# Attention's five key chunks and first 64 queries weighed in one stretch, and one copy of q moved to ScalarE

## The chip, the cores and the metric

The program runs on one core of a Trainium2 chip. The metric is the device time of one execution in microseconds (us), as a median over runs. TensorE (PE) multiplies, VectorE (DVE), ScalarE (ACT) and GpSimd (POOL) do the element work, and SyncE (SP) issues most of the DMAs. Each engine works off its own queue in the order in which the program was written, and waits for the others through semaphores.

## The reference

Three layers follow each other. The change lies in the first one alone.

```python
scores = (1.0 / np.sqrt(D)) * np.matmul(q, k.transpose(0, 1, 3, 2))   # B, H, S, D = 4, 8, 576, 64
mask = (pos[:, None] // 64) >= (pos[None, :] // 64)                   # causal by blocks of 64
scores = np.where(mask, scores, -1e9)
scores = scores - np.max(scores, axis=-1, keepdims=True)
attn = np.exp(scores)
attn = attn / (np.sum(attn, axis=-1, keepdims=True) + 1e-09)
x = np.matmul(attn, v)                     # then laid out as [B*S, H*D] = [2304, 512]
...                                        # mixture of 8 experts: each token goes to its argmax expert
...                                        # last layer: x @ w_in, a piecewise activation, @ w_out
```

## The kernel before, in words

Attention works on 16 pairs of heads, pair n = 0 to 15 (batch n // 4, two heads at a time, one head per half of the 128 partitions). Each pair goes through seven steps z = 0 to 6. Step z of pair n computes the scores of one piece of queries (`scores`), reduces their maximum on DVE and takes the exponential on ACT (`soft`, lines 344, 339 and 348 for the maximum, 350 for the exponential into `pall`). Two steps later (`LAG = 2`) `flip` transposes that piece on PE (line 368) into a PSUM tile `pt`, and ACT (line 379) or DVE (line 511) copies it to `pT`. So the last two pieces of a pair are flipped in steps 0 and 1 of the next pair. The piece that is flipped last, in step 1, is copied by ACT.

Work that is not part of this chain is placed by the table `PLAN`: its key (z, at) names the step and the place in it, `act` runs what is listed there.

```python
PLAN = {(1, 0): ["rows", "q"], (2, 0): ["sum"], (2, 2): ["k", (0, 3)], (3, 0): ["rows"],
        (4, 2): [(3, 5)], (5, 0): ["first"], (5, 1): ["store"], (6, 2): ["rows"]}
```

- "q" is `load_q` of the next pair: PE transposes q (`psq`), ACT copies it out scaled (`qT`, line 256) and casts it (`qa`, line 259, two halves); DVE (lines 265, 266) and POOL (lines 263, 260, 267, 268) make the further forms of q. Line 266 is a copy of 64 columns on 64 partitions.
- "k" is `load_k` of the next pair: PE transposes k (`psk`), DVE copies it out (`kT`, line 286) and casts two parts of `kd` (line 297), ACT casts the two others (line 295), POOL subtracts the low part `kl` in two halves (line 298).
- a pair of numbers is `weigh` of the pair before: for these chunks of 128 keys PE multiplies `pT` with v into `px` (line 393), the two heads in the two halves of the 128 output partitions, each matmul as two passes in the trace. Chunk 0 covers 512 queries, the others 448, 320, 192 and 64.
- "first" is `weigh_first` of the pair before: the first 64 queries against chunk 0 (`py`, line 408, in a tile of the two `pt` buffers), then, where the pair before is odd, `row_order`, and a copy on ACT (line 412). `row_order` is small copies of the reciprocal row sums on DVE (line 429, one or two; line 435, two).
- "sum" (DVE lines 417 and 418), "store" (ACT line 398, which empties `px`) and "rows" (PE line 445, DVE lines 451 and 455) finish the rows of the pairs before.

An even pair n is one in which the pair before is odd, so it carries "sum" and `row_order`; that is n = 2, 4, 6, 8, 10, 12 and 14. Where the batch of the pair before is odd (n = 6, 8, 14) line 429 runs twice, else once. Pairs 14 and 15 also carry the routing of the experts on DVE. After attention come the experts and the last layer, which make up the other three quarters of the time.

Of the kernel before, what the change touches and what calls it, by code (L numbers as in the profile page):

```python
# [49 lines left out]


ORDER_FIRST, ORDER_LAST, ORDER = (2, 4, 0, 1, 5, 6, 3), (3, 1, 4, 2, 6, 0, 5), (3, 1, 0, 4, 2, 6, 5)
PLAN = {(1, 0): ["rows", "q"], (2, 0): ["sum"], (2, 2): ["k", (0, 3)], (3, 0): ["rows"],
        (4, 2): [(3, 5)], (5, 0): ["first"], (5, 1): ["store"], (6, 2): ["rows"]}
FROM = 0, 128, 256, 320, 448
LAG = 2
COPY = 4
# [65 lines left out]
def attention(late, weights, tc, q, k, v, ids, w_gate, mbias, x_dram, dram, ident, tabs):  # L123
# [3 lines left out]
    nc = tc.nc  # L127
# [54 lines left out]
    def turned(dst, x):  # L182
        if x.dtype == F32R:
            nc.tensor.transpose(dst.bitcast(F32R), x, identr)
        else:
            nc.tensor.transpose(dst, x, ident)
# [58 lines left out]
    def eng(n, x):  # L245
        return nc.gpsimd if SMALL[n > 0][x] == 2 else nc.vector

    def load_q(n):
        psq = ps2.tile([P, 1024], F32, tag="big", name=f"psq{n}")
        psq = psq[:, 64:64 + S]  # L250
        for t, x in enumerate(FROM):
            turned(psq[:, x:x + P], io_t[n, "q"][:, t, :])
        qa, qb, qf = qas[n % 2], qbs[n % 2], qfs[n % 2]

        qT = wk.tile([P, 9, 64], F32, tag="qT", name=f"qT{n}", bufs=1)
        nc.scalar.activation(qT, psq.rearrange("p (i t) -> p i t", t=64), AF.Copy, scale=D ** -0.5)
        for h in range(2):
            hs, oh = slice(h * 64, h * 64 + 64), slice(64 - h * 64, 128 - h * 64)
            nc.scalar.copy(qa[hs, h, :7], qT[hs, 2:])
            eng(n, h).tensor_tensor(qa[oh, h, :7], qT[hs, 2:], qa[hs, h, :7].bitcast(F32), op=ALU.subtract)  # L260
        for h in range(2):
            hs = slice(h * 64, h * 64 + 64)
            (nc.gpsimd.tensor_copy if n else nc.scalar.copy)(
                qf[hs, h].rearrange("p (i t) -> p i t", t=64), qT[hs, :2])
        eng(n, 4).tensor_copy(qb[:64, :7], qa[:64, 0, :7])
        eng(n, 5).tensor_copy(qb[64:, 7], qa[64:, 1, 6])
        eng(n, 6).tensor_copy(qb[64:, 8:], qa[64:, 1, :6])
        eng(n, 7).tensor_copy(qzs[n % 2][:, 64:], qa[:, 1, 6])

# [199 lines left out]
    def act(n, z, at):  # L469

        if n >= B * NP:
            return
        for what in PLAN.get((z, at), ()):
            if what == "q" and n + 1 < B * NP:
                load_q(n + 1)
            elif what == "k" and n + 1 < B * NP:
                load_k(n + 1)
            elif what == "rows" and todo:
                done.add(todo[0])
                rows(*todo.pop(0))  # L480
            elif n == 0:
                continue
            elif isinstance(what, tuple):
                weigh(n - 1, *what)
            elif what == "sum" and (n - 1) % 2:
                row_sums((n - 1) // NP, (n - 1) % NP // 2)
            elif what == "first":
                weigh_first(n - 1)
            elif what == "store":
                store_xT(n - 1)  # L490
                if (n - 1) % 2:
                    todo.extend((j, (n - 1) % NP // 2) for j in rows_of[(n - 1) // NP])

    warm(WARM[0])
    load_k(0)
    load_q(0)
    warm(WARM[1])
    for g in range(len(steps) + LAG):
        n, z = divmod(g, NK)
# [1081 lines left out]
```

## Time and profile before

| what | value |
|---|---|
| median of 3 runs | 840.74 us (840.67 to 841.1) |
| the profiled execution | 839.69 us |
| its span, first to last instruction | 837.8 us |
| granted TensorE clock, mean | 0.992 |
| PE, PEld, DVE, ACT, POOL busy | 98%, 85%, 73%, 59%, 25% |
| chain that ended last | PE in 46% of the span, DVE, issue and DVE's sequencer 0% |

The times of runs are device times; the rows of the trace count from the first instruction of the profiled execution. PEld is the weight load of TensorE, which overlaps its matmuls. A matmul's end is modelled, so the distance between the starts of two matmuls tells more than their durations. Where a row says x5, five instructions of the same kind were merged, and the second number is the time from the first start to the last end.

### The profile page before, as it was taken

To read this page: it belongs to the slowest core of one execution; us is meant where nothing else is said; L and a number is where in the kernel's file an instruction comes from. 1 tells how busy PE (TensorE), PEld (TensorE's weight loads), DVE (VectorE), ACT (ScalarE), POOL (GpSimd) and SP (SyncE) were. 2 spreads that over 40 slices of the span, in tenths; PEclk is the share of its full clock that TensorE was granted. 3 is DMA by queue.
4 is the path that set the end of the run, shared out by engine and by line. 5 is a ranking of instruction groups with operands and counts; after the bars stand their busy time and mean duration, and the time that the engine had idled before them with its cause. 6 is when DMAs were issued, how large, how long until landed. Compare 5 with 4: busy or idle time off the path is not lost. (4 is left out here: it accounts for less than half of the span.)

```text
span 837.8 us, 13997 instructions
## 1 busy us (share of the span) xinstructions
PE 817.9 (98%) x4936; PEld 709.3 (85%) x4936; DVE 608.3 (73%) x1115; ACT 495.6 (59%) x994; POOL 205.4 (25%) x249
## 2 busy tenths in 40 slices
PE   6999999998899999999999999999999999999998
PEld 5777777775788888888888999999999988888887
DVE  6788888789666656797873766766636877777774
ACT  5898888896533334464544666766657644444442
POOL 8546556546301212120202000110000011112120
PEclk6999999999999999999999999999999999999999
DMA  6445655630744447765625453453644633333301
GB/s 155 119 125 144 172 145 134 171 95 20 247 131 150 153 125 234 240 204 163 203 84 162 142 176 121 170 175 134 218 120 160 239 143 128 125 126 126 132 32 38
DMA packets 138058, 123.17 MB, mean 147 GB/s; under 512 B 70183, under 2 KB 122423, under 8 KB 135296
## 3 DMA queue, kind: packets, MB, share of 16 engines
q1 hardware_dynamic: 132256, 107.98, 41.9%
q0 software_dynamic: 4384, 13.92, 4.7%
q8 instruction: 40, 0.66, 0.3%
q10 hardware_dynamic: 1344, 0.33, 0.2%
q14 instruction: 34, 0.28, 0.1%
HBM read 89.17 MB, written 40.37 MB: 155 GB/s over the span
## 5 line engine op out<-in xcount | busy, mean ns | idle before, releaser
L1019 PE MATMUL h<-yhi,wi 128*128 128x384 f32 x768 | 200.4, 338 | 1.1 <-ACTq L1253 1.1
L1019 PEld LDWEIGHTS h<-yhi,wi 128*128 128x128 f32 x768 | 139.5, 188 | 1.5 <-ACTq L1253 1.5
L1019 PE MATMUL h<-ylo,wi 128*128 128x384 f32 x384 | 129.2, 337 | 0.0
L1293 ACT ACTIVATE cl<-h,half 128x384 f32<-128x384 f32 x96 | 55.9, 582 | 69.4 <-PE h L1019 69.1
L350 ACT ACTIVATE pall<-s,nmax 128x384 f32<-128x384 f32 (+2 forms) x144 | 79.5, 558 | 28.1 <-DVE nmax L344 17.0
L1297 DVE SCALAR_TENSOR_TENSOR gg<-cl,h 128x384 f32<-128x384 f32 x96 | 52.3, 552 | 51.8 <-ACT cl L1294 49.7
L1423 PE MATMUL p<-wo,s 128*128 128x256 f32 (+1 forms) x432 | 87.8, 338 | 0.0
L1423 PEld LDWEIGHTS p<-wo,s 128*128 128x128 f32 x432 | 68.5, 188 | 9.2
L1478 POOL DMA_INDIRECT out_dram<-rest,tab x16 | 27.3, 1707 | 190.9 <-DVE rest L1445 185.4
L1019 PEld LDWEIGHTS h<-ylo,wi 128*128 128x128 f32 x384 | 72.1, 188 | 0.0
L368 PE MATMUL pt<-ident,pall 128*128 128x128 f32 x400 | 65.7, 282 | 5.5 <-DVE pT L511 3.5
L1423 PE MATMUL p<-wo,a 128*128 128x256 f32 (+1 forms) x330 | 66.0, 335 | 0.0
L1019 PE MATMUL h<-xhi,wh 128*128 128x512 f32 (+2 forms) x164 | 63.1, 385 | 0.0
L1019 PE MATMUL h<-xhi,wl 128*128 128x512 f32 (+2 forms) x164 | 61.7, 376 | 0.5 <-DVE wl L1103 0.5
L1019 PE MATMUL h<-xlo,wh 128*128 128x512 f32 (+2 forms) x164 | 61.6, 376 | 0.0
L1128 PE MATMUL acc<-wh,hl 128*128 128x512 f32 x152 | 59.6, 392 | 0.1
L1423 PEld LDWEIGHTS p<-wo,a 128*128 128x128 f32 x330 | 52.8, 188 | 7.9
L1128 PE MATMUL acc<-wl,hh 128*128 128x512 f32 x152 | 59.3, 390 | 0.0
L1128 PE MATMUL acc<-wh,hh 128*128 128x512 f32 x152 | 59.1, 389 | 0.0
L393 PE MATMUL px<-pT,v 128*64 128x448 f32 (+4 forms) x320 | 54.5, 432 | 0.0
L1294 ACT ACTIVATE cl<-cl 128x384 f32<-128x384 f32 x96 | 50.5, 526 | 3.0
L368 PEld LDWEIGHTS pt<-ident,pall 128*128 128x128 f32 x400 | 43.9, 143 | 7.0 <-issue 3.1
(316 smaller groups left out, 1807.8 us busy)
## 6 DMA issues: line engine op xcount, KB each, us to landing
raw<-in_moe_w_dram SPq DMA_DIRECT2D x80, 256.0 KB
g_dram<-gg SPq DMA_DIRECT2D x48, 384.0 KB
g<-g_dram SPq DMA_DIRECT2D x18, 1024.0 KB
wi_raw<-in_moe_w_in_dram SPq DMA_DIRECT2D x16, 512.0 KB
wo_raw<-in_moe_w_out_dram SPq DMA_DIRECT2D x16, 512.0 KB
yr<-y_dram SPq DMA_DIRECT2D x18, 256.0 KB
x_dram<-xrow SPq DMA_DIRECT2D x33, 128.0 KB
v<-in_v_dram SPq DMA_DIRECT2D x32, 128.0 KB
```

What stands on the lines that cost most here:

```text
L350: nc.scalar.activation(pall[n % 2][:, o:o + w], pss[:, u:u + w], AF.Exp, bias=nm[:, x:x + 1], scale=1.0, accum_out=ssum[:, b, c, x:x + 1])
L368: nc.tensor.transpose(pt[:, kk, :], pa[:, o + kk * P:o + (kk + 1) * P], ident)
L393: nc.tensor.matmul(pxs[n][h * 64:(h + 1) * 64, s0 - 64:], io_t[n, "v"][:, kk, h * D:(h + 1) * D], pTs[n][:, kk, h, s0:], start=(kk == 0), ...
L1019: nc.tensor.matmul(ps, a[za], b[zb], start=(i == 0), stop=(i == n - 1))
L1128: nc.tensor.matmul(accs[s][u], a[:, us], b[:, 1, :], start=(f == 0 and i == 0), stop=(f == NF - 1 and i == 2))
L1293: nc.scalar.activation(cl, ph, AF.Relu, bias=half, scale=0.5)
L1294: nc.scalar.activation(cl, cl, AF.Square)
L1297: nc.vector.scalar_tensor_tensor(gg[:, :, f % 2, :], cl.rearrange(t3, t=P), 1.0, ph.rearrange(t3, t=P), op0=ALU.min, op1=ALU.max)
L1423: nc.tensor.matmul(o, a, b, start=(x == 0 and i in FRESH), stop=(x == len(terms) - 1), skip_group_check=True)
L1478: outs.append(nc.gpsimd.indirect_dma_start(out=out[:, :], out_offset=bass.IndirectOffsetOnAxis(ap=tabs.tab[:, j, 0:1].bitcast(U32), axis=0 ...
```

## The change

`PLAN` moves three things: chunks 3 and 4 of `weigh` go from step 4 to step 2, behind chunks 0 to 2; `weigh_first` goes from the start of step 5 to step 2, ahead of `weigh`, and takes `row_order` with it; `store` goes from step 5 to step 3. In `load_q` of all pairs but the first, line 266 goes from DVE to ACT.

```diff
-PLAN = {(1, 0): ["rows", "q"], (2, 0): ["sum"], (2, 2): ["k", (0, 3)], (3, 0): ["rows"],
-        (4, 2): [(3, 5)], (5, 0): ["first"], (5, 1): ["store"], (6, 2): ["rows"]}
+PLAN = {(1, 0): ["rows", "q"], (2, 0): ["sum"], (2, 2): ["k", "first", (0, 5)], (3, 0): ["rows"],
+        (3, 1): ["store"], (6, 2): ["rows"]}
...
         eng(n, 4).tensor_copy(qb[:64, :7], qa[:64, 0, :7])
-        eng(n, 5).tensor_copy(qb[64:, 7], qa[64:, 1, 6])
+        (nc.scalar.copy if n else nc.vector.tensor_copy)(qb[64:, 7], qa[64:, 1, 6])
         eng(n, 6).tensor_copy(qb[64:, 8:], qa[64:, 1, :6])
```

On PE, step 2 of pair 5 to the scores of step 3 (the names carry buffer numbers: psk and px as above, xr the "rows", s_4 the scores of step 3). Before:

```order
L184 MATMUL psk_1149<-identr,k_892 128x128 x5
L393 MATMUL px_1165<-pT_962,v_563 64x512 x2
L393 MATMUL px_1165<-pT_962,v_563 64x448 x2
L393 MATMUL px_1165<-pT_962,v_563 64x320 x2
L445 MATMUL xr_1_1176<-rh,xT 128x144 x2
```

And now:

```order
L184 MATMUL psk_1149<-identr,k_892 128x128 x5
L408 MATMUL py_1165<-pT_962,v_563 64x64 x2
L393 MATMUL px_1169<-pT_962,v_563 64x512 x2
L393 MATMUL px_1169<-pT_962,v_563 64x448 x2
L393 MATMUL px_1169<-pT_962,v_563 64x320 x2
L393 MATMUL px_1169<-pT_962,v_563 64x192 x2
L393 MATMUL px_1169<-pT_962,v_563 64x64 x2
L445 MATMUL xr_1_1184<-rh,xT 128x144 x2
```

All matmuls with 64 output columns of weights stand together now, py ahead; the later stretch of them in step 4 and 5 is gone.

On DVE, the even pair 6 from k's copy to the maximum of its last piece (rt is what `row_order` writes):

```order
 L286 COPY kT_1389<-psk_1383 128x576
 L297 CAST kd_1391<-kT_1389 64x576 x2
-L348 TENSOR_REDUCE nmax_1257<-s_4_1410 128x1
-L511 COPY pT_1374<-pt_1_0_1414 128x2x2x128
-L348 TENSOR_REDUCE nmax_1257<-s_2_1422 128x1
 L429 COPY rt<-rinv 64x4x4 x2
 L435 COPY rt<-rinv 64x2 x2
-L339 TENSOR_REDUCE nmax_1257<-s_6_1444 128x1
+L348 TENSOR_REDUCE nmax_1257<-s_4_1422 128x1
+L511 COPY pT_1374<-pt_1_0_1427 128x2x2x128
+L348 TENSOR_REDUCE nmax_1257<-s_2_1435 128x1
+L339 TENSOR_REDUCE nmax_1257<-s_6_1445 128x1
```

The copies of `row_order` now follow the casts of kd directly, and the maxima of three pieces and a copy of pT stand behind them.

On ACT, two places of step 1 to step 4, pair 6 (pT_1140 is copied in the flip of step 1, which `weigh` waits for). Line 266 now stands between the casts of qa and that copy:

```order
 L256 ACTIVATE qT_1341<-psq_1335 128x576
 L259 CAST qa_137<-qT_1341 64x448 x2
+L266 COPY qb_139<-qa_137 64x64
 L379 COPY pT_1140<-pt_5_0_1359 128x4x128
 L350 ACTIVATE pall_157,ssum<-s_1_1353,nmax_1257 128x256 x2
```

And the two copies into xT (lines 412 and 398) now precede the exponential of step 3 instead of following that of step 4. POOL's queue is unchanged; on SP only buffer numbers differ.

## Rows read from the trace of the kernel before

**Rows 1.** Busy time in stretches: length, PE, PEld, DVE, ACT, POOL, clock, DMA share, GB/s.
```profile
26.00:187.00 161.00, 159.86 (x1231) 121.46 (x1230) 131.69 (x282) 140.50 (x389) 90.63 (x108) 1.00 0.53 136
187.00:222.00 35.00, 28.47 (x237) 21.08 (x238) 28.92 (x92) 21.28 (x58) 19.90 (x28) 1.00 0.38 120
```

**Rows 2.** Timeline of PE in the odd pair 7: start, length, what.
```profile
101.78 2.76 PE L393 MATMUL px<-pT,v 128*64 128x512 f32 x12
...
106.44 0.41 PE L368 MATMUL pt<-ident,pall 128*128 128x128 f32 x2
106.78 0.66 PE L393 MATMUL px<-pT,v 128*64 128x192 f32 x8
...
107.49 0.40 PE L316 MATMUL s<-kd,qa 128*128 128x288 f32 x1
107.73 0.29 PE L316 MATMUL s<-kd,qz 128*128 128x288 f32 x1
107.86 0.29 PE L316 MATMUL s<-kl,qb 128*128 128x288 f32 x1
```

**Rows 3.** Timeline of TensorE's weight loads there; in brackets the idle time before.
```profile
102.17 0.22 PEld L393 LDWEIGHTS px<-pT,v 128*64 128x64 f32 x3 [0.21 <-ACT pT L379]
```

**Rows 4.** Timeline of PE in pair 15.
```profile
205.67 2.37 PE L393 MATMUL px<-pT,v 128*64 128x512 f32 x12
```

**Rows 5.** Timeline of ACT in pair 7.
```profile
108.13 0.20 ACT L412 COPY xT<-py 128x64 f32<-128x64 f32 x1
108.23 0.60 ACT L398 COPY xT<-px 128x512 f32<-128x512 f32 x1
```

**Rows 6.** Timeline of DVE in the even pair 8.
```profile
113.56 0.39 DVE L265 CAST qb<-qa 64x448 fp32r<-64x448 f32 x1 [0.96 <-ACT qa L259]
114.15 0.85 DVE L266 CAST qb<-qa 64x64 fp32r<-64x64 f32 x1 [0.20 <-ACT qa L259]
...
115.75 0.43 DVE L417 TENSOR_SCALAR rinv<-ssum 128x18 f32<-128x18 f32 x1
...
117.45 0.94 DVE L297 CAST kd<-kT 64x576 fp32r<-64x576 f32 x2
118.31 0.68 DVE L348 TENSOR_REDUCE nmax<-s 128x1 f32<-128x512 f32 x1
...
120.09 1.32 DVE L429 COPY rt<-rinv 64x16 f32<-64x16 f32 x2
```

**Rows 7.** Timeline of POOL in pair 8.
```profile
113.71 2.44 POOL L260 TENSOR_TENSOR qa<-qT,qa 64x448 fp32r<-64x448 f32 x2
116.21 0.50 POOL L267 CAST qb<-qa 64x384 fp32r<-64x384 f32 x1
...
118.05 3.10 POOL L298 TENSOR_TENSOR kl<-kT,kd 64x576 fp32r<-64x576 f32 x2 [1.04 <-DVE kd L297]
```

**Rows 8.** Timeline of PE in pair 8: the first 64 queries, the flip of step 5.
```profile
119.64 0.34 PE L408 MATMUL py<-pT,v 128*64 128x64 f32 x4
...
120.81 0.60 PE L368 MATMUL pt<-ident,pall 128*128 128x128 f32 x4
```

**Rows 9.** The copies of lines 429 and 435: ns min/median/max, first and last start.
```profile
L429 DVE COPY rt<-rinv x12: 175/643/1116, 45.0 to 219.2; 64x16 f32<-64x16 f32 x8, 128x16 f32<-128x16 f32 x4
L435 DVE COPY rt<-rinv x16: 151/164/168, 46.0 to 219.6; 64x2 f32<-64x2 f32 x16
```

**Rows 10.** Timeline of PE in pair 0 and in step 0 of pair 7.
```profile
17.93 0.58 PE L326 MATMUL s<-kd,qa 128*128 128x256 f32 x1 [0.72 <-ACT pall L350]
...
97.94 0.33 PE L368 MATMUL pt<-ident,pall 128*128 128x128 f32 x1 [0.33 <-ACT pall L350]
```

**Rows 11.** Timeline of DVE in pair 14, and POOL's kl there.
```profile
194.95 0.94 DVE L297 CAST kd<-kT 64x576 fp32r<-64x576 f32 x2
...
197.84 0.93 DVE L690 TENSOR_TENSOR rk<-rk,oh 128x104 f32<-128x104 f32 x1
...
195.56 3.08 POOL L298 TENSOR_TENSOR kl<-kT,kd 64x576 fp32r<-64x576 f32 x2 [3.51 <-DVE kd L297]
```

## The prediction, before the changed kernel was run

> **What bounds the kernel now.** I read the busy time in stretches first. [...] In the last two pairs (187 to 222 us) PE is busy for 28.5 of 35 us and DVE for 28.9 [rows 1]: there DVE holds PE up.
>
> Next, PE's timeline in an odd pair. The starts show that "busy" hides losses. The two heads of px run side by side in the two halves of the array. In pair 7 the first head's first matmul starts at 101.78 [rows 2], but the second head's weights load only at 102.17, after ACT's copy of pT [rows 3]. The second head ends 0.39 us late and the next work waits for it. So the start of the stretch already hangs on ACT's chain from psq through qT and qa to that copy. The second thing to see is what a stretch of px costs at its edges. Two transposes start at 106.44; by their length, 0.41 for two of 0.27, their spacing is 0.14, and a third would start by 106.69. Instead px, py and the edges last until 107.49, and the first matmul after takes 0.24 to the next, where the one after takes 0.13 [rows 2]: 0.80 + 0.11 = 0.91 us.
>
> Last, DVE, POOL and PE in an even pair. On DVE, the copy of line 266 takes 0.85 us and ends at 115.00, just behind POOL's first subtract (half of 2.44 from 113.71, so 114.93); line 417 ends at 116.18, behind the second (116.15). Line 429 starts at 120.09 and its two copies take 1.32 us, though one alone takes 0.18: POOL's kl runs from 118.05 to 121.15, and the first copy ends only then [rows 6, 7, 9]. So a DVE copy from SBUF to SBUF waits for the POOL instruction that is running, until it ends. Maxima, which read PSUM, do not: that of 118.31 runs its 0.68 us beside kl [rows 6].
>
> **The change, part by part.** The sum is made against the profiled execution (839.69 us), which is 1.05 us below the median of 840.74.
>
> *One stretch instead of two.* The later stretch of 0.91 us goes; its 320 columns per head (192 + 64 of px, 64 of py) now run inside the first. A stretch in which neither head waits takes 2.37 us for 512 + 448 + 320 = 1280 columns with its edges [rows 4], 1.85 ns a column, so they cost at most 0.59. Gain 0.3 us a pair, for pairs 1 to 15.
>
> *py ahead of px.* py takes the `pt` buffer that ACT's copy in step 1 empties, so now both heads wait for it, where only the second did. Since the second head set the end, this costs nothing further. *Line 266 on ACT* stands ahead of that copy and delays it. No row shows it on ACT. The nearest is ACT's copy of 64 columns, line 412: 0.20 us long, 0.10 from its start to that of the next [rows 5]. I take 0.10; the bounds are 0 and 0.28 (one full copy and a hand-over). A gain is excluded, as ACT's queue ahead of it is unchanged.
> Odd pairs 1 to 13: 7 x (-0.3 + 0.1) = **-1.4**. Pair 15 has no later q: **-0.3**.
>
> *The copy off DVE.* In the odd pairs the maxima come up to 0.85 us earlier, and PE waits for none of them. In pair 0 it does: PE idles 0.72 us at 17.93 for an exponential whose maximum stood behind line 266 [rows 10]: **-0.7**.
>
> *The store earlier* empties px sooner; nobody waits for it. Its two copies on ACT, 0.7 us [rows 5], now precede the exponential of step 3, which must wait for later matmuls and a maximum anyway: nothing. DMA issues and POOL's queue do not move.
>
> *row_order in step 2.* This is the dear part. Take pair 8. Without line 266, DVE goes on at 113.95 instead of 115.00, and line 417 waits for POOL's first subtract instead of the second, ending at 114.98 instead of 116.18. What follows moves 1.2 us up to the casts of kd, due at 116.25 instead of 117.45. There POOL runs line 267 (116.21 to 116.71), so the first cast ends near 117.0, the second near 117.5 [rows 6, 7]. kl starts 0.14 after the end of the first cast (118.05 against 117.45 + 0.46), so near 117.15, and its halves of 1.55 us end at 118.7 and 120.25. Line 429 is due at 117.5 and waits for the first half. POOL goes on at once with the second, so the next copy waits for that: 120.3. Two of 0.16 follow: 120.65. Behind them in DVE's queue stands the maximum of step 3, 0.68 us, which now starts at 118.31 [rows 6]; then ACT's exponential, 0.69 by the same number of columns, and hand-overs of 0.1: 122.1. PE's flip of that piece, which started at 120.81 [rows 8], starts 1.3 us later. What PE gains before that point is lost in this wait: the stretch joined, and the 0.3 us by which py ran late in this pair, at 119.64 behind DVE's copy of pT [rows 8]. Pairs 6 and 8 have two copies of line 429: 2 x 1.3. Pairs 2, 4, 10 and 12 have one; the second small copy of line 435 is then the one that meets the second half, and 0.3 us of copies less stands behind it: 4 x 1.0. Sum **+6.6**. What line 429 costs now in step 0 of the next pair, 0.33 us at 97.94 [rows 10] and less in others, goes: **-0.5**.
>
> *Pair 14* has no POOL work beside row_order now, and will have: the casts end at 195.89, kl at 198.64 [rows 11]. With DVE 0.4 earlier the copies end near 198.5, and the next maximum comes 2.7 later than the 195.8 at which it follows the casts now. Given back are 0.7 of copies that stood later and some 0.65 of line 690's 0.93, of which most is the wait for kl [rows 11]: **+1.3**, with bounds of 0 and 2.7.
>
> Sum: -1.4 - 0.3 - 0.7 + 6.6 - 0.5 + 1.3 = **+5.0 us**, so 844.7 by the profiled execution and 845.7 by the median. The chain of pair 8 is worked with no slack at all and a few tenths of it can overlap; I take 0.1 off each of seven pairs: **845.0 us**. After attention PE is the bound up to the end, and what PE loses reaches the end.
>
> [...] The small copies of line 435 never met POOL: all sixteen took 0.15 to 0.17 us [rows 9]. That they wait like line 429 is my reading, by the nearest row: the same operation between the same two tiles. [...] If only what rows show holds, the four pairs with one line 429 fall to the second rival below. [...]
>
> **The rivals.** *First, faster: the copies wait once.* If the rest of the copies slips in between kl's halves, before POOL takes up the second, the maximum of pair 8 starts at 118.7 + 0.04 + 0.5 = 119.25 and the flip at 120.75, even with now; in the four pairs with one line 429 it is 0.2 better than now; pair 14 comes out even. Sum: -1.4 - 0.3 - 0.7 - 0.8 - 0.1 - 0.5 = -3.8, 837 us. For it: a copy that is waiting could bring the next along before POOL goes on. Against: line 417 and line 266, each behind a POOL instruction, show POOL going on at once. It decides by when that maximum starts: PE would reach the flip at about 120.3 (120.81 less 0.3 and 0.3, plus 0.1), and 1.5 us of maximum, exponential and hand-overs lie before it, so from 118.8 on each tenth of delay is a tenth of PE's time.
>
> *Second: only the small copies of line 435 pass.* Then pairs 2, 4, 10 and 12 gain 0.2 instead of losing 1.0: 4.8 less, 840.2 us.
>
> *Third: line 266 on ACT costs 0.28.* The odd pairs lose their gain: 7 x 0.18 = +1.3, 846.3 us.
>
> *Fourth: the loss is taken up later*, in the 35 us where DVE holds PE up [rows 1]: about 841 us. Against: DVE's work of those pairs hangs on the same scores and comes late with them.
>
> **How the numbers follow.** Forecast 0.62, copies wait once 0.16, small copies pass 0.11, ACT dearer 0.05, taken up 0.06. The forecast's own range is 842 to 849: per even pair 0.6 to 1.6 in place of 1.0 to 1.3 (6 x 0.4 either way), pair 14 between 0 and 2.7. The second and fourth rivals lie within 839 to 842; the first, at 837, stays out. So 838.5 to 849.0. A measurement of this kernel can tell about 0.2% from no change, 1.7 us. Faster by more (below 839.1): the first rival and a little of the second, 0.19. Within it (up to 842.4): most of the second and fourth, 0.16. Slower: the forecast and the third, 0.65.
>
> **What would show it.** In the changed profile of pair 8: line 429 merged with a length near 2.5 us or more directly behind the casts of kd, both halves of kl under it; an idle time on PE of 1 to 2 us before a transpose of line 368, put down to ACT's pall, in every even pair; periods of odd pairs 0.2 us shorter; py right behind psk, waiting for ACT's pT. Wrong would be: rt's copies short, or long with no idle PE behind them, or even pairs no longer than now.

## The result, and the profile after

| | before | after |
|---|---|---|
| median | 840.7 us (840.62 to 841.1, 4 runs) | 846.21 us (845.03 to 847.9, 4 runs) |
| profiled execution, its span | 839.69 us, 837.8 us | 847.9 us, 846.1 us |
| granted TensorE clock, mean | 0.992 | 0.988 |
| PE, DVE, ACT, POOL busy | 98%, 73%, 59%, 25% | 96%, 72%, 59%, 24% |

The changed kernel takes 1.0066 times the time of the kernel before (95% interval 1.0049 to 1.0082): slower by 5.5 us. The sum of the prediction was 5.0; its forecast, with 0.7 taken off for overlap, was 845.0 us, 4.3 above the kernel before. The execution whose trace is read below is the longest of the four, 1.7 us above their median.

The busy time in the two stretches of [rows 1], in the changed kernel:

```profile
26.00:187.00 161.00, 144.74 (x1171) 111.72 (x1171) 128.66 (x254) 137.50 (x386) 86.74 (x105) 0.99 0.52 135
187.00:222.00 35.00, 29.98 (x253) 23.53 (x252) 30.91 (x89) 22.64 (x64) 18.68 (x28) 0.90 0.16 49
```

PE, the bound of attention before, now lacks 16.3 of 161 us, and its mean granted clock is no longer 1.00. The two groups of copies of [rows 9] show why (minimum, median, maximum in ns):

```profile
L429 DVE COPY rt<-rinv x12: 176/1292/1307, 40.6 to 226.0; 64x16 f32<-64x16 f32 x8, 128x16 f32<-128x16 f32 x4
L435 DVE COPY rt<-rinv x16: 151/167/1409, 41.8 to 226.4; 64x2 f32<-64x2 f32 x16
```

The median of line 429 doubled, and line 435, never above 0.17 us before, now reaches 1.41. DVE's timeline in pair 8, to be laid beside [rows 6], and POOL's beside [rows 7]:

```profile
114.33 0.39 DVE L265 CAST qb<-qa 64x448 fp32r<-64x448 f32 x1 [0.96 <-ACT qa L259]
114.64 0.68 DVE L344 TENSOR_REDUCE nmax<-s 128x2 f32<-128x512 f32 x1
115.25 0.51 DVE L417 TENSOR_SCALAR rinv<-ssum 128x18 f32<-128x18 f32 x1
...
117.02 1.27 DVE L297 CAST kd<-kT 64x576 fp32r<-64x576 f32 x2
118.30 1.51 DVE L429 COPY rt<-rinv 64x16 f32<-64x16 f32 x2
119.85 1.45 DVE L435 COPY rt<-rinv 64x2 f32<-64x2 f32 x2
121.33 0.69 DVE L348 TENSOR_REDUCE nmax<-s 128x1 f32<-128x512 f32 x1
```

```profile
114.48 2.44 POOL L260 TENSOR_TENSOR qa<-qT,qa 64x448 fp32r<-64x448 f32 x2
...
117.98 3.11 POOL L298 TENSOR_TENSOR kl<-kT,kd 64x576 fp32r<-64x576 f32 x2
```

Four small copies fill 118.30 to 121.30, as long as kl runs on POOL, and the maximum behind them starts only then. PE's timeline of that pair shows who pays, to be laid beside [rows 8]:

```profile
112.32 0.63 PE L184 MATMUL psq<-identr,q 128*128 128x128 f32 x5
...
121.08 0.29 PE L316 MATMUL s<-kl,qb 128*128 128x288 f32 x1
122.88 0.66 PE L368 MATMUL pt<-ident,pall 128*128 128x128 f32 x4 [1.51 <-ACT pall L350]
123.47 0.23 PE L635 MATMUL idp<-ident,idf 18*128 18x18 f32 x1
123.84 0.67 PE L326 MATMUL s<-kd,qa 128*128 128x512 f32 x1
...
128.27 0.63 PE L184 MATMUL psq<-identr,q 128*128 128x128 f32 x5
```

The flip of step 5, at work without a wait before, stands idle for 1.51 us. The same view of line 368 alone, over 26 to 187 us, has six such waits, one in each of the pairs 2, 4, 6, 8, 10 and 12 (before there were two, 0.6 us together, the larger in [rows 10]):

```profile
L368 PE MATMUL pt<-ident,pall x300: 270/273/455, 30.0 to 182.2; 128*128 128x128 f32 x150
its engine sat idle before it (us, times) until:
  ACT pall L350: 7.7, 6
```

In an odd pair the two other parts of the change can be seen, the copy of line 266 on ACT and the joined stretch. ACT's and PE's timelines of pair 7, for [rows 2, 3]:

```profile
100.51 0.65 ACT L256 ACTIVATE qT<-psq 128x576 f32<-128x576 f32 x1 [0.20 <-PE psq L184]
101.19 1.15 ACT L259 CAST qa<-qT 64x448 fp32r<-64x448 f32 x2
102.38 0.24 ACT L266 CAST qb<-qa 64x64 fp32r<-64x64 f32 x1
102.64 0.59 ACT L379 COPY pT<-pt 128x512 f32<-128x512 f32 x1
```

```profile
103.28 0.34 PE L408 MATMUL py<-pT,v 128*64 128x64 f32 x4 [0.61 <-ACT pT L379]
103.45 2.76 PE L393 MATMUL px<-pT,v 128*64 128x512 f32 x20
```

The copy of line 266 takes 0.24 us on ACT and moves the copy of pT by 0.26 (102.38 to 102.64). PE waits for that copy ahead of py, and then runs all five chunks in one piece.

One thing in the profile after was in no step of the prediction. Three stretches of pair 8, with the granted clock in the third column from the right:

```profile
122.00:124.00 2.00, 0.98 (x6) 0.72 (x7) 1.92 (x5) 1.93 (x6) 0.00 (x0) 1.00 0.72 225
124.00:126.00 2.00, 2.00 (x9) 1.48 (x10) 0.69 (x1) 1.26 (x4) 1.51 (x4) 0.50 0.37 148
126.00:128.00 2.00, 2.00 (x13) 1.69 (x12) 1.10 (x4) 0.90 (x3) 0.00 (x0) 0.65 0.00 1
```

Behind the idle 1.51 us the clock is at its lower level, 0.50 of full speed, for 3.41 us from 124.0 on; it is there again from 202.5 (6.83 us) and from 226.4 (3.41 us). From 26 us to the end of attention the kernel before was never at that level (1.00 in both stretches of [rows 1]).

### The profile page after: what moved, and what is told of

Same layout as the page of the kernel before. It is cut to its first block, busy times and chain, and to the rows that moved or that the text cites. A ratio compares the mean times of both kernels' runs of the same rounds, so it can differ in the third digit from the quotient of the medians.

```text
span 846.1 us, 14025 instructions
## 1 busy us (share of the span) xinstructions
PE 810.0 (96%) x4936; PEld 704.0 (83%) x4936; DVE 612.5 (72%) x1100; ACT 499.5 (59%) x1009; POOL 204.8 (24%) x249
## 5 line engine op out<-in xcount | busy, mean ns | idle before, releaser
L1100 ACT CAST wh<-raw 128x1024 fp32r<-128x1024 f32 x40 | 41.9, 1051 | 13.2 <-PE acc L1128 13.1
```

Of the source, the lines that this page charges most:

```text
L1100: nc.scalar.copy(ws[s, f][0], weights.raw[s, f])
```

## The experiments

A pair's period, from the start of the turns of q (line 184) to the next such start, separates the effects better than the total. The table gives it in us for the pairs that alternate. Pairs 6 and 8 stand apart because line 429 has two copies there, pairs 7 and 9 because their periods differ from the other odd ones in the kernel before already. "Idle" is PE's idle time ahead of py and ahead of line 368 between 26 and 187 us; by the kernel's pace 12 to 14 pairs start their stretch in that window. "-" is a value that is left out, as the lower clock falls into it.

| kernel | pairs 3, 5, 11, 13 | 7, 9 | 2, 4, 10, 12 | 6 | 8 | idle py | idle 368 |
|---|---|---|---|---|---|---|---|
| before | 12.12 to 12.13 | 12.61 | 12.47 to 12.64 | 13.11 | 12.94 | 0 | 0.6 |
| after | 12.07 | 12.55 | 13.44 to 13.61 | 13.95 | 15.95 | 8.3 | 7.7 |
| e1 | 12.06 | 12.55 | 12.05 to 12.21 | 12.58 | 12.53 | 8.9 | 0.2 |
| e2 | 11.80 | 12.28 | 14.31 (pair 10) | - | - | 4.3 | 11.2 |
| e3 | 12.39 to 12.41 | 12.89 | 12.39 to 12.56 | 12.55 | 12.76 | 0 | 0 |
| e4 | 12.06 | 12.54 | 12.05 to 12.22 | 12.33 | 12.64 | 8.9 | 0 |
| e5 | 11.78 to 11.81 | 12.28 | 12.48 to 12.63 | 13.10 | 12.95 | 4.6 | 0.9 |
| e6 | 12.34 (13: 12.61) | 12.82 | 13.45 to 13.61 | 13.95 | 14.33 | 12.1 | 6.0 |
| e7 | 11.79 to 11.80 | 12.28 | 11.79 to 11.95 | 12.31 | 12.24 | 5.2 | 0.2 |
| e8 | 12.87 to 12.88 | 12.97 | 13.53 to 13.62 | 14.11 | 14.07 | 0 | 4.0 |
| e9 | 11.68 to 11.69 | 12.15 to 12.16 | 13.30 to 13.34 | 13.81 | 13.76 | 0 | 8.0 |

The kernel before ran beside each group, each group on a chip of its own: 840.48 us for e1 to e4, 837.25 for e5 to e8, 841.08 for e7 once more and e9. Ratios are taken against these. The times expected of e5 to e8 were worked out from runs beside 840.5 to 840.7 us, so there the periods are the better test.

**e1: row_order back at the start of step 5.** Everything else of the change stays.

```diff
-        (3, 1): ["store"], (6, 2): ["rows"]}
+        (3, 1): ["store"], (5, 0): ["order"], (6, 2): ["rows"]}
...
-                weigh_first(n - 1)
+                weigh_first(n - 1, False)
+            elif what == "order":
+                if (n - 1) % 2:
+                    row_order((n - 1) // NP, (n - 1) % NP // 2)
```

> The change with row_order alone put back to the start of step 5. If the even pairs lose their time to row_order's copies behind kl (the theory), their idle time of 1.2 to 1.5 us on PE before the flip of step 5 is gone; even pairs come out some 0.3 us shorter than in the kernel before and odd ones 0.05 shorter, so with the 1 to 1.6 us of pair 0 and 1 some 836 to 838 us. If the loss came from the joined stretch, or from the store and the copy of q on ACT (the rival), nothing changes: 845 to 847 us.

Measured: 833.72 us (832.69 to 834.19), ratio 0.9913 (0.99 to 0.9926). The waits of line 368 are gone but for one, and the copies run at their own length:

```profile
L368 PE MATMUL pt<-ident,pall x325: 270/273/329, 30.0 to 183.9; 128*128 128x128 f32 x163
its engine sat idle before it (us, times) until:
  ACT pall L350: 0.2, 1
```

```profile
L429 DVE COPY rt<-rinv x12: 176/178/183, 43.6 to 212.9; 64x16 f32<-64x16 f32 x8, 128x16 f32<-128x16 f32 x4
L435 DVE COPY rt<-rinv x16: 153/164/167, 43.7 to 213.2; 64x2 f32<-64x2 f32 x16
```

What follows: the copies of row_order, where they stand, are the whole loss and more, and the rest of the change gains. Each even pair is 1.4 us shorter than in the changed kernel (pair 8 by 1.8 against its 14.33 at the full clock in e6), and the mean granted clock of this execution is 1.000 over its 832.0 us. The gain of the rest, 6.8 us, is above the 2.5 to 4.5 that I expected; e3 and e5 split it.

**e2: the new order alone, line 266 back on VectorE.**

```diff
-        (nc.scalar.copy if n else nc.vector.tensor_copy)(qb[64:, 7], qa[64:, 1, 6])
+        eng(n, 5).tensor_copy(qb[64:, 7], qa[64:, 1, 6])
```

> The new table alone, line 266 on DVE as before. By the theory the copy on DVE delays the casts of kd, so kl and row_order's copies come up to 0.9 us later: even pairs lose 1.9 us instead of 1.0, odd pairs gain 0.3; 849 to 852 us. If the copy on ACT is what costs the time (the rival), this is faster than the change: below 845 us.

Measured: 859.75 us (857.62 to 861.43), ratio 1.0225 (1.0207 to 1.0244), worse than the 849 to 852 expected. The waits ahead of the flip of step 5 are longer, 2.10 to 2.45 us, as DVE comes to row_order later. Pair 10, the one even pair from 2 to 12 that ran wholly at the full clock, lost 1.84 us against the kernel before, and 1.9 was expected; what was not expected is the clock. It falls to 0.50 for 3.41 or 6.83 us seven times between 48.0 and 239.1 us (mean of the execution 0.984), five of them in or right behind such a wait. PE's timeline of pair 6, and the stretch behind it:

```profile
103.28 1.11 PE L368 MATMUL pt<-ident,pall 128*128 128x128 f32 x4 [2.45 <-ACT pall L350]
```

```profile
104.00:108.00 4.00, 4.00 (x18) 3.17 (x17) 1.62 (x5) 2.66 (x8) 0.00 (x0) 0.50 0.00 0
```

**e3: line 266 on ScalarE alone, in the old order.**

```diff
-        eng(n, 5).tensor_copy(qb[64:, 7], qa[64:, 1, 6])
+        (nc.scalar.copy if n else nc.vector.tensor_copy)(qb[64:, 7], qa[64:, 1, 6])
```

> The table as before, line 266 on ACT. The copy lies ahead of the copy of pT that the second head waits for: 0.26 us in each odd pair, some 0.1 us gained in each even one where DVE is freed, 0.7 to 1.6 us gained in pair 0 and 1: 840 to 842 us. If the rival holds (the copy is what makes the change slow), 844 to 846 us.

Measured: 839.31 us (837.9 to 841.25), ratio 0.9987 (0.9976 to 0.9997), 0.7 below the theory's window and far from the rival's. Odd pairs are 0.27 us longer, even pairs 0.08 shorter (pair 6 by 0.56, pair 8 by 0.18).

**e4: row_order in step 2 as in the change, but ahead of load_k.**

> The change with row_order still in step 2, but ahead of load_k, so its copies meet POOL's short instructions of q and the casts of kd and kl follow them. By the theory it is kl that they must not stand behind: they wait at most 1 us in all, kd comes about 1 us later, and the maximum of step 3 at most 0.5 us late; 836 to 840 us, no idle time on PE of over 0.6 us before the flip of step 5. If any copies of row_order ahead of that maximum cost the time, wherever they stand (the rival), 845 to 847 us.

The edit puts "order" between the sums and "k" of step 2. Measured: 833.45 us (831.93 to 834.99), ratio 0.9911 (0.9896 to 0.9925), with nearly the periods of e1 and 2.5 us better than the theory's 836 at best. Line 429 takes up to 0.73 us here too, but no flip waits behind it (idle 368 is 0). So it is not the step that costs, but the place behind the casts of kd, for which POOL's kl waits (1.04 us in [rows 7]).

**e5: the joined stretch alone** (e1 with line 266 back on VectorE, the edit of e2).

> The join alone: the five chunks and the first 64 queries in one stretch at step 3, the six copies of row_order left at the start of step 5 as before, and line 266 back on VectorE. Theory (the copy of line 266 costs ScalarE's chain some 0.26 us in each pair that hangs on the copy of pT, but takes work from VectorE where POOL stands beside it, so it costs and gains about the same): odd pairs near 11.8 us or 0.25 below those of the change, even pairs some 0.1 to 0.4 us above 12.1, 832 to 837 us. Rival 1 (the copy on ScalarE is a plain loss, since even pairs hang on ScalarE and TensorE too): every pair 0.26 us shorter than with the copy, 829 to 831 us. Rival 2 (the copy on ScalarE is what frees VectorE in even pairs, the join alone brings little): 838 to 841 us.

Measured: 835.13 us (834.43 to 836.92), ratio 0.9978 (0.9968 to 0.9987). The theory's window held; beside a kernel before of 837.25 us that is a gain of 2.1. The odd pairs are 0.32 us shorter than before: that is the join, as the prediction priced it (0.3). The even pairs are as long as before. The row of line 429 says where the join's gain goes there:

```profile
L429 DVE COPY rt<-rinv x12: 176/605/983, 44.7 to 213.7; 64x16 f32<-64x16 f32 x8, 128x16 f32<-128x16 f32 x4
```

In each even pair from 2 to 12 its first copy takes 0.96 to 0.98 us, as kl still runs when DVE comes to it in step 5; in e1, with the same table, it takes 0.18. A flip behind it then waits for ACT's exponential, 0.13 to 0.15 us in pairs 2, 4, 10 and 12 and 0.62 in pair 6. That these waits are all that the join loses was not shown. With e3 this splits the change. In odd pairs -0.32 and +0.27 add up to the -0.05 seen. In pairs 2, 4, 10 and 12 the join alone gives 0.0 and the copy alone -0.08, but both (e1) -0.42: the join pays there only once DVE is rid of line 266. Pair 8 is alike (0.0, -0.18, -0.41); in pair 6 the copy alone gives it all (0.0, -0.56, -0.53).

**e6: the changed kernel with the copy of line 266 issued twice on ScalarE.**

```diff
+        if n:
+            nc.scalar.copy(qb[64:, 7], qa[64:, 1, 6])
```

> The changed kernel with line 266's 64-column copy issued twice on ScalarE (the second writes the same values again). Theory (each such copy stands ahead of ScalarE's copy of pT in step 1, for which the first 64 queries wait; odd pairs hang on it, even pairs on VectorE's copies behind kl): odd pairs 0.24 to 0.26 us longer (near 12.3), even pairs the same, 847 to 849 us. Rival (all pairs hang on ScalarE): 0.25 us in each of 14 pairs, 849.5 to 851 us. Second rival (the copy is hidden beside TensorE's work): 846 to 846.5 us.

Measured: 846.8 us (844.48 to 847.38), ratio 1.0104 (1.0086 to 1.0123). The time lies just under the theory's window, beside a faster kernel before; the periods are the theory's: odd pairs +0.27 (pair 13 +0.54), even pairs the same. The total is 0.4% above the changed kernel's by the two ratios, 3.2 us, whose intervals just miss each other (1.0082 and 1.0086); seven odd pairs make 2.2 of it. ACT's timeline shows the price of one copy once more, 0.27 from start to start:

```profile
103.76 0.24 ACT L266 CAST qb<-qa 64x64 fp32r<-64x64 f32 x1
104.03 0.24 ACT L268 CAST qb<-qa 64x64 fp32r<-64x64 f32 x1
104.30 0.59 ACT L381 COPY pT<-pt 128x512 f32<-128x512 f32 x1
```

It also prices the clock. In this execution pair 8 ran wholly at a granted clock of 1.00 and took 14.33 us, against 15.95 in the changed kernel: the 3.41 us at 0.50 cost 1.62 there.

**e7: as e1, with the copy of line 266 issued at the end of step 1,** behind ScalarE's copy of pT.

```diff
-PLAN = {(1, 0): ["rows", "q"], (2, 0): ["sum"],
+PLAN = {(1, 0): ["rows", "q"], (1, 2): ["late"], (2, 0): ["sum"],
...
-        (nc.scalar.copy if n else nc.vector.tensor_copy)(qb[64:, 7], qa[64:, 1, 6])
+        if not n:
+            nc.vector.tensor_copy(qb[64:, 7], qa[64:, 1, 6])
...
+            elif what == "late" and n + 1 < B * NP:
+                nc.scalar.copy(qbs[(n + 1) % 2][64:, 7], qas[(n + 1) % 2][64:, 1, 6])
```

> The join with row_order at step 5 as before, and line 266 on ScalarE, but issued at the end of step 1, behind the copy of pT and the exponentials of that step. Theory (in its old place the copy delays the copy of pT by 0.26 us and TensorE's weights of the first 64 queries with it; behind it costs nothing): the waits of py 0.26 us shorter (0.25 to 0.5 us left), 13 pairs by 0.2 to 0.26 us, 830 to 831.5 us. Rival (what the copy of pT gains is given back at the next wait, VectorE's in even pairs): only odd pairs gain, 832 to 833 us; or nothing, 833.5 us.

Measured: 829.82 us (828.79 to 831.3), ratio 0.991 (0.9894 to 0.9925). Every pair from 1 to 13 is 0.26 to 0.29 us shorter than in e1, so even pairs gain too and the rival falls, and PE's idle time ahead of py fell from 8.9 to 5.2 us. The view of py's line:

```profile
L409 PE MATMUL py<-pT,v x56: 222/246/271, 26.7 to 182.1; 128*64 128x64 f32 x56
its engine sat idle before it (us, times) until:
  ACT pT L380: 5.2, 14
```

> The kernel with line 266's copy behind step 1 once more, beside the next one on the same chip. As before: odd pairs 11.8 us, even pairs 11.9 to 12.0 (pairs 6, 7, 8 and 9 near 12.3), 828 to 832 us.

Once more, on another chip: 830.9 us (830.18 to 833.08), ratio 0.9878 (0.9859 to 0.9898), with the same periods. This version beats both kernels. That it beats e1 rests on the periods: by the totals only the second run is clear of e1's ratio (0.9913), the first (0.991) is not.

**e8: as e1, with all of load_q at the end of step 1.** The edit moves "q" from (1, 0) to (1, 2).

> As the run with row_order at step 5, but with the whole of load_q (TensorE's turns of q, ScalarE's scaled copy, the casts, line 266) at the end of step 1 in place of its start, so that the copies of pT come ahead of it on ScalarE. Theory (TensorE's wait of 0.5 to 0.8 us ahead of the first 64 queries is the ScalarE queue's, nothing else): that wait goes in 13 or 14 pairs, 14 x 0.6 = 8.4 us less than 833.7, 824 to 828 us. Rival (q comes late then: VectorE's residues and copies of line 260 to 266 are pushed into kl's stretch beside POOL and the next pair's scores wait for them): even and odd pairs 12.2 to 13, 833 to 842 us.

Measured: 849.17 us (847.98 to 851.6), ratio 1.0145 (1.0124 to 1.0166), above both windows. The wait ahead of py is gone, but another has taken its place, which neither theory named: the turns of k wait until ACT has read the turned q, 0.86 us in a pair.

```profile
L184 PE MATMUL psk<-identr,k x50: 244/250/283, 54.1 to 174.4; 128*128 128x128 f32 x50
its engine sat idle before it (us, times) until:
  ACT qT L256: 8.6, 10
```

**e9: as e7, with only the casts to qa and what follows them at the end of step 1.** The part of load_q from line 258 on becomes a function that is called there.

> As the kernel with line 266's copy behind step 1, but with only TensorE's turns of q and ScalarE's scaled copy qT left at the start of step 1: the two casts to qa and all that follows them (the residues, qf, qb, line 266) are issued at the end of the step. TensorE's turns of k wait for qT alone, which stays where it was, so the wait of the run with all of load_q at the end should not come back. Theory: the copy of pT comes two casts (some 0.5 us) earlier, the waits ahead of py (0.32 and 0.49 us) go in 13 pairs, 4 to 6 us less than the run beside it, 824 to 827 us. Rival: VectorE's residues and POOL's copies of q now start later and meet kT, kd and kl in step 2; the even pairs, and perhaps all, lose what py gains: the same to 6 us more, 829 to 836 us.

Measured: 841.22 us (839.69 to 842.94), ratio 1.0001 (0.999 to 1.0011). The rival was right in kind, though the time lies 5 us above its window: the wait ahead of py is gone and odd pairs gain 0.1 us (11.69), but even pairs lose 1.4 (13.3). VectorE meets GpSimd there again. In pair 4 line 417 takes 1.10 us, 0.50 in e7, and line 429 takes 1.12, 0.18 in e7, and the flips wait twice in that pair, 0.69 and 0.71 us. ScalarE's copy of pT cannot be had earlier for nothing in either way that was tried.

## Why the prediction was right

The chain of pair 8 is the core of it, and it came out to a tenth of a microsecond. The turns of q start at 111.55 before and 112.32 after, so 0.77 is taken off the times after. Line 429 then starts at 117.53 (forecast 117.5), the maximum of step 3 at 120.56 (120.65), the flip of step 5 at 122.11 (122.1).

- *One stretch instead of two*, 0.3 us: 0.32 in the odd pairs (e5). (By the spacing of 0.14 that the working names, the third transpose would start at 106.72 and not at 106.69; the term would still be 0.3.) That py waits for ACT's copy of pT costs nothing beyond, as said: the wait ahead of it is large (0.61 us in pair 7), and yet the pair is shorter (12.55 us instead of 12.61).
- *Line 266 on ACT*, taken as 0.10 with 0.28 as the upper bound: **this term was mis-sized.** It measured 0.26, so that the third rival was right in its price (0.28). I had chosen the 0.10 from the start of line 412's copy to that of the next [rows 5], which overlap; behind qa's casts (up to 102.34 in pair 7) and ahead of pT's copy (from 102.64) there is no overlap, and the whole copy counts (102.38 to 102.62). The seven odd pairs 1 to 13 gave 0.53 us instead of 1.4. The fifteen copies on ACT took 0.241 to 0.243 us; the whole 0.20 of line 412's copy would have been a better price than 0.10.
- *row_order in step 2, with the relief of line 429 in step 0*, 6.6 - 0.5 = 6.1 us: the six even pairs lost 0.97, 0.97, 0.84, 1.39 (pair 8 as e6 shows it at the full clock), 0.97 and 0.97, together 6.1. The way was a little different. In pair 8 the first copy of line 429 waits for kl's first half, the second slips through, and it is the first copy of line 435 that waits for the second half. One trace row for each line shows it (minimum, median, maximum in ns):

```profile
L429 DVE COPY rt<-rinv x2: 178/740/1303, 118.3 to 119.6; 64x16 f32<-64x16 f32 x2
...
L435 DVE COPY rt<-rinv x2: 167/718/1269, 119.8 to 121.1; 64x2 f32<-64x2 f32 x2
```

- So the first rival, that the rest slips in between the halves, had one copy's worth of truth: of the copies behind the first one passes, not all. In the pairs with one line 429 it is the second copy of line 435 that waits, as forecast. The second rival falls: the small copies of line 435 do wait (1.27 here, 1.40 in the pairs with one line 429).
- *Pair 0*, 0.7: at about the same clock (6.83 us at 0.50 in the changed kernel, from 8.0 on; by its mean of 0.996 over 832.6 us some 6.7 in all of e5) the kernels with and without the copy on DVE differ by 1.2 us there (turns of q of pair 1 at 24.22 in e5, 23.05 after). PE's idle time there is 1.80 us in e5 and 0.70 after; the 0.72 of [rows 10] was smaller because PE ran at 0.50 ahead of it, from 7.7 us on, and came later. So the term was sized from an idle time that a low clock had shortened. Against the kernel before, the turns of q of pair 1 start 1.64 earlier; the clock, which rose from 0.50 to 1.00 at 14.8 us instead of 21.4, has a part in that.
- *Pairs 14 and 15*, 1.3 - 0.3: from the last turns of q to the start of the last matmul of px 38.25 us instead of 35.77. Of the 2.48 us PE's idle time is 0.57. The rest is busy time, and 10.2 us of the stretch ran at 0.50, so that the term can't be checked closely. The copies met kl there as in the other pairs:

```profile
200.77 1.48 DVE L429 COPY rt<-rinv 64x16 f32<-64x16 f32 x2
202.27 1.44 DVE L435 COPY rt<-rinv 64x2 f32<-64x2 f32 x2
```

- *Not taken up later*: the last matmul of px starts at 230.25 instead of 222.23, 8.0 us late, and the span is 8.3 us longer. So the fourth rival did not come true; what the last two pairs would have done without the lower clock no run shows.

The parts of the profiled executions sum to -1.64 - 0.53 + 6.1 + 1.62 + 2.48 + 0.27 (behind px) = 8.3 us. The sum's 5.0 differs from that by the lower clock, 1.62 in pair 8 and a part of the 2.48, and by the odd pairs, with the first 25 us against it. The median of the runs lies only 5.5 us above before. That it came so near the forecast is in part luck. The odd pairs gave 0.9 less than their term and the start up to 0.9 more. The 0.7 taken off for overlap did not come, as the even pairs lost the whole sum. And the falls of the clock stood in no term. What the prediction had right by its working is the chain of the even pairs and the price of the join.

Of the signs that were named, two came out: PE's idle time of 1 to 2 us in every even pair, put down to ACT's pall, and py right behind psk with its wait for pT. Two did not: line 429 did not reach 2.5 us in pair 8 but 1.51, as line 435 took the other wait (1.45), and the odd pairs became 0.05 us shorter, not 0.2.

What stays open is when the clock falls. In the changed kernel it fell behind the idle 1.51 us of pair 8, and did not behind the 1.52 of pair 6:

```profile
96.56 0.66 PE L368 MATMUL pt<-ident,pall 128*128 128x128 f32 x4 [1.52 <-ACT pall L350]
```

With idles of 2.1 to 2.45 us (e2) it fell five times in six.

## What to carry to other kernels

Before small VectorE copies are moved, look at what GpSimd runs at their new place: here the price was the rest of its instruction, paid again for the next one that GpSimd had in line (1.30 and 1.27 us in pair 8), and it fell on what stood behind the copies in VectorE's queue (the flip's wait of 1.51 us). The same copies cost some 12.5 us more right behind the casts, beside kl, than ahead of the casts (e4) or in step 5 once kl is over by then (e1), the clock's falls among them. In step 5 of e5, where kl is not over, line 429 still waits. Price a copy that goes into the queue of an engine on the critical chain by its whole length (0.24 us here, which cost 0.26), unless rows show that it overlaps both neighbours there; and then try it behind the instruction that others wait for, which here made each pair from 1 to 13 another 0.26 to 0.29 us shorter (e7).

## What was not expected of the hardware

- In pair 8 the VectorE copy that had waited for the first half of GpSimd's kl let one more through behind it (0.18 us) before the second half shut the following out: 1.30, 0.18, 1.27 and 0.17 us for the four copies, each of 0.15 to 0.18 in e1, where they stand in step 5. In pair 4, with three, it was 1.30, 0.15 and 1.40.
- Idle times of 1.5 to 2.5 us on TensorE were at times followed by 3.41 or 6.83 us at a granted clock of 0.50, in the changed kernel after 109 us at 1.00. In pair 8 that cost 1.62 us, more than the wait itself (1.51). Pairs 2, 4 and 12 of e2 lost 1.61 to 1.63 us more than its pair 10, with 3.41 us at 0.50 in each.
- The two gains depend on each other: in pairs 2, 4, 10 and 12 joining the stretch gave nothing, taking the copy off VectorE 0.08 us, and both together 0.42.
